# RWKV-5 attention and a two-layer MLP on one core: second MLP product by a seven-product scheme in six of twelve pairs, and joined masks

## The chip, the cores and the metric

The kernel runs on one core of one Trainium2 chip. The metric is device time in microseconds. Before the change, three runs took 173.43, 173.54 and 174.15 us; their median is 173.54 us.

## The reference

Inputs are r, k, v of shape 4 x 8 x 768 x 48 (batch, head, token, channel), a decay w and a bonus u per head and channel, and the MLP's matrices `w_in` (384 x 2048) and `w_out` (2048 x 384). All is float32; the kernel works in bfloat16 with float32 sums.

```python
for t in range(S):                       # S = 768
    cur = einsum('bhd,bhe->bhde', u * k[t], v[t])
    y[t] = einsum('bhd,bhde->bhe', r[t], state + cur)
    state = w * state + einsum('bhd,bhe->bhde', k[t], v[t])
x = y.transpose(0, 2, 1, 3).reshape(3072, 384)
h = x @ w_in                             # 3072 x 2048
out = maximum(0.01 * h, h) @ w_out       # 3072 x 384
```

## The kernel before

The 3072 tokens are cut into 24 stages of 128 tokens; six stages make one batch (NC = 6), so the running state starts anew at stages 0, 6, 12 and 18. Two stages form a pair, and there are twelve pairs, 0 to 11. Work is written as a list of operations with the tiles that each reads and writes (`Sched.add`); each engine plays its own operations in that order, and semaphores are put in between engines where one needs another's result, or where a buffer is still being read.

**What one stage does.** `load_one` (L210) loads r, k and v by DMAs that POOL issues. `prep` (L305, L307) multiplies r and k by tables of powers of the decay on VectorE (DVE), into `qk`; from stage 8 on SP then issues a DMA that transposes `qk` into `tp` (L310), while earlier stages are turned on TensorE (`turn`, L355). `prep2` makes the bonus term: from stage 8 on it multiplies twice and reduces on DVE (L330, L332, L334), and POOL writes two diagonal tiles into `at` (L342); for earlier stages it scales v (`vs`, L325). `a_mm` (L377) multiplies queries and keys into two PSUM banks, one for each half of the heads; `a_mask` puts the part below the diagonal into `at` with one DVE operation for each bank (L387, or L391 as a predicated copy over the diagonal tiles). `kv_mm` (L408) and `state` (L458, or L461 and L463) carry the state on, the latter on DVE. `y_part` (L493) sums everything into the output in small matmuls of 32 columns of the array; for stages below 8, twelve of them add `vs` through the identity. ScalarE (ACT) copies the result into `xT` (L508).

**The MLP.** `g1_pair` (L538) multiplies `w_in` by a pair's `xT`, 256 tokens at a time, in eight groups of six matmuls; ACT applies the leaky maximum and writes `gT` (L544). `g2` (L555) multiplies one stage's `gT` by `w_out`: 16 matmuls of 384 columns into one PSUM bank. ACT copies it out (L561), and SP stores the stage (L563).

**Order.** Stages 0 to 9 and the first pairs of the MLP follow a list written by hand (`ORDER`), in which J is `g1_pair`, H is `g2`, P `prep`, Q `prep2`, A `a_mm`, M `a_mask`, K `kv_mm`, S `state`, Y `y_part`, L the loads. Then a loop runs over m = 3 to 11 (L576 to L604). One turn m holds the eight `g1_pair` of pair m; `prep2` of stages 2m+4 and 2m+5; loads of 2m+8 and 2m+9; `a_mm` and `a_mask` of 2m+4 and 2m+5; `y_part` of 2m+2 and 2m+3; `kv_mm` and `state` of 2m+4 and 2m+5 (not of a batch's last stage); `prep` of 2m+6 and 2m+7; and `g2` of both stages of pair m-1. The two `g2` of pair 11 stand behind the loop.

**PSUM.** There are eight banks of 512 columns, taken round in turn by `next_bank`: a new user of a bank waits until the readers of the user eight banks earlier are done. In the turn m = 5, for example, the sixteen takers before `g2` are eight `g1_pair`, four halves of `a_mm`, two `y_part` and two `kv_mm`, so that the first `g2` gets the bank of the first half of `a_mm(14)`.

Of the kernel before, what the change touches and what calls it, by code (L numbers as in the profile page):

```python
# [5 lines left out]
ALU = mybir.AluOpType  # L6
# [114 lines left out]
def bass_rwkv5_eagle__then__act_leaky_relu_kernel(  # L121
# [32 lines left out]
    qtab = SB("qtab", [128, HD])  # L154
    ktab = SB("ktab", [128, HD])
# [21 lines left out]
    gT = [SB(f"gT{i}", [128, NFB, 256]) for i in range(NG)]  # L177
    out_sb = [SB(f"out_sb{i}", [128, HD], FP32) for i in range(NO)]
    ps = [ctx.enter_context(nc.psum_tensor(f"ps{i}", [128, 512], FP32)) for i in range(8)]
# [22 lines left out]
    def load_one(n, which, pace=()):  # L202
# [3 lines left out]
        if which == "v":  # L206
            dst = v_sb[:, n, :].rearrange("p (h e) -> p h e", e=E)[:, :, 0:D]
        else:
            dst = {"k": k_sb, "r": r_sb}[which][:, n, :].rearrange("p (h d) -> p h d", d=D)
        add("pool", lambda: G.dma_start(dst, src), R=pace, W=[(which, n)], dma=f"{which}{n}")  # L210

# [85 lines left out]
    def k_of(n):  # L297
        return k_sb[:, n, :] if n else k0_f[:, :]

    def r_of(n):  # L300
        return r_sb[:, n, :] if n else r0_f[:, :]
# [12 lines left out]

# [5 lines left out]
    def prep2(n):  # L320
# [8 lines left out]
        else:  # L329
            add("dve", lambda: V.tensor_tensor(ku[i2][:, :], k_of(n), u_tab[:, :], ALU.mult),  # L330
                R=[("k", n), "u_tab"], W=[("ku", i2)])
            add("dve", lambda: V.tensor_tensor(rku[i2][:, :], r_of(n), ku[i2][:, :], ALU.mult),  # L332
                R=[("r", n), ("ku", i2)], W=[("rku", i2)])
# [35 lines left out]
    def a_mm(n):  # L369
        it = n % NTP  # L370
        at_bank[n] = (next_bank(), next_bank())
# [11 lines left out]
    def a_mask(n):  # L383
        for hh in range(2):
            part = at_bank[n][hh][0][:, :].rearrange("p (m i) -> p m i", i=128)
            if n < DIAG:
                add("dve", lambda hh=hh, part=part: V.tensor_tensor(  # L387
# [188 lines left out]
    for m in range(FIRST // 2, NST // 2):  # L576
# [3 lines left out]
        for n in ahead:  # L580
            prep2(n)
# [82 lines left out]
```

## Time and profile before

The profiled execution spans 171.8 us from the first to the last instruction; the median run of 173.54 us lies 1.7 us above that span. The granted clock of TensorE is 1.00 in every stretch up to 158 us.

| what | value |
|---|---|
| median of runs / span of the profiled execution | 173.54 us / 171.8 us |
| busy: PE, DVE, ACT, POOL | 95%, 56%, 54%, 60% of the span |
| second MLP product (L555), 384 matmuls | 64.5 us |
| first MLP product in pairs (L538), 480 matmuls | 54.5 us |
| POOL's diagonal tiles (L342), 32 | 33.8 us, 1081 ns each |
| masks (L391), 32 | 19.8 us, 684 ns each |
| last instruction of DVE | at 138.6 us |
| store of an output stage (192 KB), median to landing | 2.2 us |

In a row of the profile the columns are line, engine, operation, output<-input, shape and count; then the busy time and the mean of one instruction, which can overlap with the next. In a timeline or a chain of waits the first two columns are start and length in us, and a bracket gives the idle time before and what ended it. A matmul's mean length (326 ns at 384 columns) holds its way through the array; what one costs in a stream is seen from a run of many. PE is TensorE's matmuls, PEld its weight loads.

### The profile page before, as it was taken

The numbers are of one execution on the slowest core, as the hardware profiler recorded it, in microseconds if no ns is written. First come the engines' busy times: TensorE is split into PE (matmuls) and PEld (weight loads), VectorE is DVE, ScalarE is ACT, GpSimd is POOL, SyncE is SP. The second block draws the span as 40 slices with busy tenths as digits, with TensorE's granted clock in tenths as the row PEclk, the third lists the DMA queues.
The fourth block names the chain that finished last, engine by engine and source line by source line (L and its number), as shares of the span: only waits on it lengthen the run. The fifth ranks groups of instructions, "written<-read, shape, count | busy, mean of one in ns | idle before, by whom it ended". The sixth has DMA issues, their size and how long they took to land.

```text
span 171.8 us, 5029 instructions
## 1 busy us (share of the span) xinstructions
PE 163.4 (95%) x2179; PEld 122.4 (71%) x2179; DVE 95.7 (56%) x209; ACT 92.5 (54%) x169; POOL 102.7 (60%) x117
## 2 busy tenths in 40 slices
PE   6799999969999989999999999999999999999993
PEld 1578799859666856876877867868868768678661
DVE  7699859550999679079189197296396520000000
ACT  4755698759123841942934934825817718539121
POOL 7999999990379998972993997957207200000000
PEclk9999999999999999999999999999999999999999
DMA  5999999999999999999499499899008011011112
GB/s 98 119 150 157 171 153 173 200 179 144 112 98 240 94 145 126 202 101 116 133 93 138 128 89 143 147 116 217 0 4 214 4 46 46 4 46 50 46 48 92
DMA packets 98970, 19.66 MB, mean 114 GB/s; under 512 B 92290, under 2 KB 98948, under 8 KB 98948
## 3 DMA queue, kind: packets, MB, share of 16 engines
q0 software_dynamic: 76512, 10.03, 89.7%
q1 hardware_dynamic: 21394, 9.11, 27.1%
q8 instruction: 17, 0.28, 0.7%
q10 hardware_dynamic: 1042, 0.20, 0.6%
q14 instruction: 5, 0.04, 0.1%
HBM read 20.45 MB, written 4.72 MB: 146 GB/s over the span
## 4 chain that ended last, share of the span: by engine, by line
PE 76%; DMA 9%; DVE 6%; POOL 6%; issue 2%; ACT 0%; POOLq 0%; ACTq 0%
PE ps L555 30%; PE ps L538 28%; PE ps L521 6%; PE ps L493 6%; DMA tp<-qk 5%; DMA w_in_sb<-in_moe_w_in_dram 4%; PE ps L377 3%; PE ps L408 2%; DVE qk L307 2%; POOL v_sb L210 2%; POOL r_sb L210 2%; POOL k_sb L210 2%; PE ps L355 1%; DVE ku L330 1%; DVE s_tok L334 1%
## 5 line engine op out<-in xcount | busy, mean ns | idle before, releaser
L555 PE MATMUL ps<-w_out_sb,gT 128*128 128x384 bf16 x384 | 64.5, 326 | 0.0
L538 PE MATMUL ps<-xT,w_in_sb 128*128 128x256 bf16 x480 | 54.5, 273 | 0.0
L555 PEld LDWEIGHTS ps<-w_out_sb,gT 128*128 128x128 bf16 x384 | 36.9, 98 | 23.4
L342 POOL TENSOR_TENSOR at<-ident,s_tok 128x512 bf16<-128x512 bf16 x32 | 33.8, 1081 | 30.3 <-DVE s_tok L334 30.3
L544 ACT ACTIVATE gT<-ps 128x512 bf16<-128x512 f32 x80 | 47.8, 597 | 7.0 <-PE ps L538 2.1
L538 PEld LDWEIGHTS ps<-xT,w_in_sb 128*128 128x128 bf16 x480 | 46.7, 98 | 6.4
L561 ACT ACTIVATE out_sb<-ps 128x384 f32<-128x384 f32 x24 | 11.8, 490 | 55.1 <-PE ps L555 55.1
L391 DVE CAST_PREDICATED at<-mask,ps 128x512 bf16<-128x512 uint16 x32 | 19.8, 684 | 27.6 <-PE ps L377 25.3
L210 POOL DMA_DIRECT2D v_sb<-in_v_dram x24 | 22.6, 948 | 0.4 <-issue 0.4
L210 POOL DMA_DIRECT2D k_sb<-in_k_dram x23 | 21.7, 945 | 0.0
L210 POOL DMA_DIRECT2D r_sb<-in_r_dram x23 | 21.4, 932 | 0.0
L508 ACT ACTIVATE xT<-ps 128x384 bf16<-128x384 f32 x24 | 11.0, 490 | 4.8 <-PE ps L493 4.3
L521 PE MATMUL ps<-xT,w_in_sb 128*128 128x128 bf16 x192 | 12.3, 219 | 0.3 <-DMA w_in_sb<-in_moe_w_in_dram 0.3
L493 PE MATMUL ps<-at,v_sb 128*32 128x128 bf16 x384 | 11.9, 224 | 0.0
L521 PEld LDWEIGHTS ps<-xT,w_in_sb 128*128 128x128 bf16 x192 | 11.1, 98 | 1.0 <-DMA w_in_sb<-in_moe_w_in_dram 0.6
L526 ACT ACTIVATE gT<-ps 128x512 bf16<-128x512 f32 x16 | 9.6, 599 | 3.6 <-PE ps L521 3.0
L332 DVE TENSOR_TENSOR rku<-r_sb,ku 128x384 bf16<-128x384 bf16 x16 | 10.8, 674 | 0.5
L387 DVE TENSOR_TENSOR at<-ps,mask 128x512 bf16<-128x512 f32 x16 | 10.3, 682 | 1.3 <-PE ps L377 1.3
L493 PEld LDWEIGHTS ps<-at,v_sb 128*32 128x32 bf16 x384 | 9.1, 98 | 2.0 <-issue 0.5
L366 ACT ACTIVATE tp<-ps 128x512 bf16<-128x512 f32 x15 | 8.2, 596 | 3.8 <-PE ps L355 3.8
L493 PE MATMUL ps<-tp,st 128*32 128x128 bf16 x240 | 10.1, 219 | 0.0
L377 PE MATMUL ps<-tp 48*128 48x128 bf16 x192 | 9.1, 228 | 0.9 <-DMA tp<-qk 0.7
(62 smaller groups left out, 134.5 us busy)
## 6 DMA issues: line engine op xcount, KB each, us to landing
out_dram<-out_sb SPq DMA_DIRECT2D x24, 192.0 KB, 2.2
v_sb<-in_v_dram POOLq DMA_DIRECT2D x24, 96.0 KB, 5.9
r_sb<-in_r_dram POOLq DMA_DIRECT2D x23, 96.0 KB, 5.1
k_sb<-in_k_dram POOLq DMA_DIRECT2D x23, 96.0 KB, 5.0
w_in_sb<-in_moe_w_in_dram POOLq DMA_DIRECT2D x4, 384.0 KB, 7.4
w_out_sb<-in_moe_w_out_dram POOLq DMA_DIRECT2D x4, 384.0 KB, 11.1
tp<-qk SPq DMA_TRANSPOSE x16, 3.4
r_f<-in_r_dram SPq DMA_DIRECT2D x1, 192.0 KB, 3.5
```

Of the source, the lines that this page charges most:

```text
L210: add("pool", lambda: G.dma_start(dst, src), R=pace, W=[(which, n)], dma=f"{which}{n}")
L332: add("dve", lambda: V.tensor_tensor(rku[i2][:, :], r_of(n), ku[i2][:, :], ALU.mult), R=[("r", n), ("ku", i2)], W=[("rku", i2)])
L342: add("pool", lambda hh=hh, s_of=s_of: G.tensor_tensor(at[ia][:, hh, :, :], ident[:, :].unsqueeze(1).to_broadcast([128, NP, 128]), s_of.un ...
L377: last = PE.matmul(at_bank[n][hh][0][:, 128 * p:128 * p + 128], tp[it][rows, NP + p, :], tp[it][rows, p, :], start=True, stop=True)
L391: add("dve", lambda hh=hh, part=part: V.copy_predicated(at[n % NAT][:, hh, :, :], mask[:, :].bitcast(mybir.dt.uint16).unsqueeze(1).to_broa ...
L493: last = PE.matmul(ps_y[32 * q:32 * q + 32, 128 * s:128 * s + 128], a, m, start=first_mm, stop=last_mm)
L508: add("act", lambda: A.activation(xT[m % NX][:, :, 128 * half:128 * half + 128], ps_y[:, 0:HD].rearrange("p (s t) -> p s t", t=128), AF.Copy),
L521: last = PE.matmul(ps_g[:, 128 * f:128 * f + 128], w_in_sb[:, s, 128 * fb:128 * fb + 128], xT[ix][:, s, t], start=s == 0, stop=s == NSL - 1)
L538: last = PE.matmul(ps_g[:, 256 * f:256 * f + 256], w_in_sb[:, s, 128 * fb:128 * fb + 128], xT[ix][:, s, :], start=s == 0, stop=s == NSL - 1)
L544: add("act", lambda: A.activation(gT[ig][:, 2 * j:2 * j + 2, :].rearrange("p f t -> p (f t)"), ps_g[:, :], AF.Prelu, alpha=0.01), R=[key], ...
L555: last = PE.matmul(ps_o[:, 0:HD], gT[ig][:, s, 128 * half:128 * half + 128], w_out_sb[:, s, :], start=s == 0, stop=s == NFB - 1)
L561: add("act", lambda: A.activation(out_sb[io][:, :], ps_o[:, 0:HD], AF.Copy), R=[key], W=[("o", io)])
```

## The change

The second MLP product of a pair is, in blocks, a 2 x 2 matrix product: rows are the pair's two stages (128 tokens each), the inner dimension is cut into two halves of 1024 (`top` and `low`, eight blocks of 128 each), and the 384 output columns into two halves of 192. Done plainly, that is eight block products. For pairs 4, 6, 8, 9, 10 and 11 (`SEVEN`) it becomes seven block products of eight matmuls of 192 columns each, in the manner of Strassen and Winograd:

- `w_sum` makes four sums of blocks of `w_out` once (DVE, 1536 wide, bfloat16), two at the end of turn m = 3 and two at the end of m = 4.
- `g_sum` makes four sums of blocks of a pair's `gT` (DVE, 1024 wide, bfloat16), behind `prep2` in the turn that follows the pair; for pair 11 behind the loop.
- `g2_seven` runs the products in three banks (four for pair 11). One bank is filled, read, and added to again: by ACT (`keep`, a float32 copy of 192 columns) or by DVE (`plus`, a sum of the bank and a kept copy that gives a quarter of the output). Pair 11 has its own order and stores each quarter by itself; the other pairs store whole stages.

Beside this, from stage 8 on `prep` is one DVE operation over r and k together (768 wide); `a_mask` is one operation over both banks of a stage (1024 wide), for which `a_mm` takes two neighbouring banks and skips bank 7 where they would not be neighbours; r and k lie in a ring of 14 stages, so a load waits for the readers of the stage 14 before; and for stages below 8 the twelve small matmuls with `vs` become three over the full array. PSUM is declared as one tensor. The diff, cut to its core (declarations, keys and the output's buffers are left out):

```diff
-    NQK, NTP, NVS, NAT, NT, NX, NG, NO = 6, 6, 6, 6, 6, 3, 3, 4
+    NQK, NTP, NVS, NAT, NT, NX, NG, NO, NRK = 6, 6, 6, 6, 6, 3, 3, 4, 14
     TURNED, DIAG = 8, 8
+    SEVEN = (4,6,8,9,10,11)
+    HF, NH = NFB // 2, HD // 2
     w_in_sb = SB("w_in_sb", [128, NSL, DFF])
     w_out_sb = SB("w_out_sb", [128, NFB, HD])
-    r_sb = SB("r_sb", [128, NST, HD])
-    k_sb = SB("k_sb", [128, NST, HD])
+    rk_sb = SB("rk_sb", [128, NRK, 2, HD])
...
+    tw = [SB(f"tw{i}", [128, HF, NH]) for i in range(4)]
+    gs = [[SB(f"gs{i}_{j}", [128, HF, 128]) for j in range(4)] for i in range(2)]
+    snap = [[SB(f"snap{i}_{j}", [128, NH], FP32) for j in range(4)] for i in range(2)]
...
+    ps_all = ctx.enter_context(nc.psum_tensor("ps_all", [128, 8 * 512], FP32))
+    ps = [ps_all[:, 512 * i:512 * i + 512] for i in range(8)]
...
     def prep(n):
         iq = n % NQK
-        add("dve", lambda: V.tensor_tensor(qk[iq][:, 0:H, 0:D], hd(r_of(n)), hd(qtab[:, :]), ALU.mult),
-            R=[("r", n), "qtab", ("qk0", iq)], W=[("qp", iq)])
-        add("dve", lambda: V.tensor_tensor(qk[iq][:, H:2 * H, 0:D], hd(k_of(n)), hd(ktab[:, :]), ALU.mult),
-            R=[("k", n), "ktab", ("qk0", iq)], W=[("kp", iq)])
         if n >= TURNED:
+            both = rk_sb[:, n % NRK, :, :].rearrange("p w (h d) -> p (w h) d", d=D)
+            by = tab[:, :, :].rearrange("p w (h d) -> p (w h) d", d=D)
+            add("dve", lambda: V.tensor_tensor(qk[iq][:, :, 0:D], both, by, ALU.mult),
+                R=[("r", n % NRK), ("k", n % NRK), "qtab", "ktab", ("qk0", iq)], W=[("qp", iq), ("kp", iq)])
             add("sp", lambda: SP.dma_start_transpose(tp[n % NTP][:, :, :],
                                                      qk[iq][:, :, :].rearrange("p h e -> p (h e)")),
                 R=[("kp", iq), ("qp", iq), ("qk0", iq)], W=[("tp", n % NTP, 0), ("tp", n % NTP, 1)],
                 dma=f"tp{n % NTP}")
+            return
+        add("dve", lambda: V.tensor_tensor(qk[iq][:, 0:H, 0:D], hd(r_of(n)), hd(qtab[:, :]), ALU.mult),
+            R=[("r", n % NRK), "qtab", ("qk0", iq)], W=[("qp", iq)])
+        add("dve", lambda: V.tensor_tensor(qk[iq][:, H:2 * H, 0:D], hd(k_of(n)), hd(ktab[:, :]), ALU.mult),
+            R=[("k", n % NRK), "ktab", ("qk0", iq)], W=[("kp", iq)])
...
     def a_mm(n):
         it = n % NTP
+        if n >= DIAG and taken[0] % 8 == 7:
+            taken[0] += 1
         at_bank[n] = (next_bank(), next_bank())
...
     def a_mask(n):
+        if n >= DIAG:
+            i = at_bank[n][0][1][1]
+            halves = [("at", n % NAT, hh) for hh in range(2)]
+            add("dve", lambda: V.copy_predicated(
+                at[n % NAT][:, :, :, :].rearrange("p two m i -> p (two m) i"),
+                mask[:, :].bitcast(mybir.dt.uint16).unsqueeze(1).to_broadcast([128, H, 128]),
+                ps_all[:, 512 * i:512 * i + 1024].rearrange("p (m i) -> p m i", i=128)),
+                R=[key for _, key in at_bank[n]] + ["mask"] + halves, W=halves)
+            return
...
-                if n < DIAG:
-                    one.append((vs[iv][:, 128 * s + 32 * q:128 * s + 32 * q + 32], ident[:, :]))
...
+                                         start=first_mm and (s == 0 or n >= DIAG),
+                                         stop=last_mm and n >= DIAG)
+            if n < DIAG:
+                for s in range(NSL):
+                    last = PE.matmul(ps_y[:, 128 * s:128 * s + 128], vs[iv][:, 128 * s:128 * s + 128], ident[:, :],
+                                     start=False, stop=s == NSL - 1)
...
+    def w_sum(i):
+        top, low = slice(0, HF), slice(HF, NFB)
+        one, two = slice(0, NH), slice(NH, HD)
+        a, b, op, keys = [
+            (w_out_sb[:, top, two], w_out_sb[:, top, one], ALU.subtract, []),
+            (w_out_sb[:, low, two], tw[0][:, :, :], ALU.subtract, [("tw", 0)]),
+            (w_out_sb[:, low, two], w_out_sb[:, top, two], ALU.subtract, []),
+            (w_out_sb[:, low, one], tw[1][:, :, :], ALU.subtract, [("tw", 1)]),
+        ][i]
+        add("dve", lambda: V.tensor_tensor(tw[i][:, :, :], a, b, op),
+            R=[("wout", j) for j in range(4)] + keys, W=[("tw", i)])
+
+    def g_sum(m, i):
+        ig, x = m % NG, gs[m % 2]
+
+        def block(r, c):
+            return gT[ig][:, HF * c:HF * c + HF, 128 * r:128 * r + 128]
+
+        def held(r, c):
+            return [("gT", ig, r, j) for j in range(4 * c, 4 * c + 4)]
+
+        a, b, op, keys = [
+            (block(1, 0), block(1, 1), ALU.add, held(1, 0) + held(1, 1)),
+            (x[0][:, :, :], block(0, 0), ALU.subtract, [("gs", m % 2, 0)] + held(0, 0)),
+            (block(0, 0), block(1, 0), ALU.subtract, held(0, 0) + held(1, 0)),
+            (block(0, 1), x[1][:, :, :], ALU.subtract, [("gs", m % 2, 1)] + held(0, 1)),
+        ][i]
+        add("dve", lambda: V.tensor_tensor(x[i][:, :, :], a, b, op), R=keys, W=[("gs", m % 2, i)])
+
+    def g2_seven(m):
+        ig, i2 = m % NG, m % 2
+        final = m == NST // 2 - 1
+        banks = [next_bank() for _ in range(4 if final else 3)]
+        top, low = slice(0, HF), slice(HF, NFB)
+        one, two = slice(0, NH), slice(NH, HD)
+
+        def product(where, left, right, first, last):
+            ps_o, key = banks[where]
+            if isinstance(left, int):
+                lhs, reads = gs[i2][left], [("gs", i2, left)]
+            else:
+                r, c = left
+                lhs = gT[ig][:, HF * c:HF * c + HF, 128 * r:128 * r + 128]
+                reads = [("gT", ig, r, j) for j in range(4 * c, 4 * c + 4)]
+            if isinstance(right, int):
+                rhs = tw[right]
+                reads = reads + [("tw", right)]
+            else:
+                rhs = w_out_sb[:, right[0], right[1]]
+                reads = reads + [("wout", i) for i in range(4)]
+
+            def emit():
+                for s in range(HF):
+                    done = PE.matmul(ps_o[:, 0:NH], lhs[:, s, :], rhs[:, s, :], start=first and s == 0,
+                                     stop=s == HF - 1, skip_group_check=not (first and last))
+                return done
+
+            add("pe", emit, R=reads, W=[key])
...
+        def keep(where, i):
+            ps_o, key = banks[where]
+            add("act", lambda: A.activation(snap[i2][i][:, :], ps_o[:, 0:NH], AF.Copy), R=[key], W=[("snap", i2, i)])
...
+        def plus(where, i, r, c, after=()):
+            ps_o, key = banks[where]
+            io, cols = (2 * m + r) % NO, (one, two)[c]
+            add("dve", lambda: V.tensor_tensor(out_sb[io][:, cols], ps_o[:, 0:NH], snap[i2][i][:, :], ALU.add),
+                R=[key, ("snap", i2, i), *after], W=[("o", io, c)])
+            store(r, c)
...
+        if not final:
+            product(0, (0, 0), (top, one), True, False)
+            keep(0, 0)
+            product(1, 0, 0, True, False)
+            keep(1, 1)
+            product(0, 1, 1, False, False)
+            keep(0, 2)
+            product(2, (0, 1), (low, one), True, True)
+            plus(2, 0, 0, 0)
+            product(0, 2, 2, False, False)
+            plus(0, 1, 1, 1)
+            product(1, 3, (low, two), False, True)
+            plus(1, 2, 0, 1)
+            product(0, (1, 1), 3, False, True)
+            plain(0, 1, 0)
+            return
+        product(0, (0, 0), (top, one), True, False)
+        keep(0, 0)
+        product(3, 2, 2, True, False)
+        keep(3, 3)
+        product(2, (0, 1), (low, one), True, True)
+        plus(2, 0, 0, 0)
+        product(3, (1, 1), 3, False, True)
+        product(1, 0, 0, True, False)
+        add("dve", lambda: V.tensor_tensor(snap[i2][1][:, :], banks[1][0][:, 0:NH], snap[i2][3][:, :], ALU.add),
+            R=[banks[1][1], ("snap", i2, 3)], W=[("snap", i2, 1)])
+        product(0, 1, 1, False, True)
+        keep(0, 2)
+        plus(0, 1, 1, 1, after=[("snap", i2, 2)])
+        plus(3, 2, 1, 0)
+        product(1, 3, (low, two), False, True)
+        plus(1, 2, 0, 1)
...
+    def second(m):
+        if m in SEVEN:
+            g2_seven(m)
+        else:
+            g2(2 * m)
+            g2(2 * m + 1)
+
     for m in range(FIRST // 2, NST // 2):
         for j in range(8):
             g1_pair(m, j)
         ahead = [n for n in (2 * m + 4, 2 * m + 5) if n < NST]
         for n in ahead:
             prep2(n)
+        if m - 1 in SEVEN:
+            for i in (0, 1, 3, 2):
+                g_sum(m - 1, i)
         for n in (2 * m + 8, 2 * m + 9):
             if n < NST:
                 load_stage(n, pace=[("pace", 2 * m, 0)])
@@ -600,10 +752,13 @@
         for n in (2 * m + 6, 2 * m + 7):
             if n < NST:
                 prep(n)
-        g2(2 * m - 2)
-        g2(2 * m - 1)
-    g2(NST - 2)
-    g2(NST - 1)
+        if m < 5:
+            w_sum(2 * m - 6)
+            w_sum(2 * m - 5)
+        second(m - 1)
+    for i in (2, 0, 1, 3):
+        g_sum(NST // 2 - 1, i)
+    second(NST // 2 - 1)
```

More of the change, by code (lines that the diff above doesn't have):

```diff
@@ L153, in bass_rwkv5_eagle__then__act_leaky_relu_kernel @@
     r0_f = SB("r0_f", [128, HD], FP32)
-    qtab = SB("qtab", [128, HD])
-    ktab = SB("ktab", [128, HD])
+    tab = SB("tab", [128, 2, HD])
+    qtab, ktab = tab[:, 0, :], tab[:, 1, :]
     tcol = SB("tcol", [128, 1], FP32)
@@ L208, in load_one @@
         else:
-            dst = {"k": k_sb, "r": r_sb}[which][:, n, :].rearrange("p (h d) -> p h d", d=D)
-        add("pool", lambda: G.dma_start(dst, src), R=pace, W=[(which, n)], dma=f"{which}{n}")
+            dst = {"k": k_sb, "r": r_sb}[which][:, n % NRK, :].rearrange("p (h d) -> p h d", d=D)
+        key = (which, n if which == "v" else n % NRK)
+        add("pool", lambda: G.dma_start(dst, src), R=pace, W=[key], dma=f"{which}{n}")
     def load_stage(n, pace=()):
@@ L330, in prep2 @@
             add("dve", lambda: V.tensor_tensor(ku[i2][:, :], k_of(n), u_tab[:, :], ALU.mult),
-                R=[("k", n), "u_tab"], W=[("ku", i2)])
+                R=[("k", n % NRK), "u_tab"], W=[("ku", i2)])
             add("dve", lambda: V.tensor_tensor(rku[i2][:, :], r_of(n), ku[i2][:, :], ALU.mult),
-                R=[("r", n), ("ku", i2)], W=[("rku", i2)])
+                R=[("r", n % NRK), ("ku", i2)], W=[("rku", i2)])
             add("dve", lambda: V.tensor_reduce(s_tok[i2][:, :], hd(rku[i2][:, :]), AX.X, ALU.add),
```

40 lines of the change are left out of this document (25 added, 15 removed).

## The prediction

> **What bounds the kernel now.** I read the page first. Its slices show TensorE (PE) at nine tenths nearly everywhere, VectorE (DVE) idle at the end, GpSimd (POOL) and the DMA engines full in the first half.
>
> ```profile
> PE   6799999969999989999999999999999999999993
> DVE  7699859550999679079189197296396520000000
> POOL 7999999990379998972993997957207200000000
> L555 PE MATMUL ps<-w_out_sb,gT 128*128 128x384 bf16 x384 | 64.5, 326 | 0.0
> ```
>
> Next I read the chain that ended last, in order of time, at two places.
>
> ```profile
> 34.22 1.51 issue
> ...
> 53.12 8.41 DMA tp<-qk
> 61.53 0.14 issue
> 61.66 0.40 PE ps L377 x8
> ...
> 87.74 5.20 PE ps L555 x32
> 92.94 5.24 PE ps L538 x48
> ...
> 158.45 10.41 PE ps L555 x64
> ```
>
> From 61.66 to 168.86 the chain is PE alone: the second product of a pair of stages takes 5.20 us, the first 5.24. Before that, PE stands twice: at 34.2 for 1.5 us with no releaser (an instruction fetch is under way), and at 60.9 for 0.73 us for the transposed stage 11. So from 61 us on PE work removed is time removed, as long as no other engine becomes late. The third view, the timeline of DVE and POOL in iteration m=5, says who could be.
>
> ```profile
> 80.29 0.35 DVE L330 TENSOR_TENSOR ku<-k_sb,u_tab 128x384 bf16<-128x384 bf16 x1
> 80.67 1.08 DVE L332 TENSOR_TENSOR rku<-r_sb,ku 128x384 bf16<-128x384 bf16 x1
> 81.79 0.55 DVE L334 TENSOR_REDUCE s_tok<-rku 128x8 f32<-128x384 bf16 x1
> 86.45 2.48 DVE L391 CAST_PREDICATED at<-mask,ps 128x512 bf16<-128x512 uint16 x4 [4.11 <-PE ps L377]
> 80.46 4.20 POOL L342 TENSOR_TENSOR at<-ident,s_tok 128x512 bf16<-128x512 bf16 x4 [4.20 <-DVE s_tok L334]
> ```
>
> DVE has a hole of 4.11 us (82.3 to 86.4), where the change puts its sums. But rku, 0.36 us one stage earlier, takes 1.08 us: it ends 0.21 us after the first POOL product, as if the two could not run together. Reductions and sums with a PSUM operand beside POOL keep their length.
>
> **Durations.** The PE step is 5.20/32 = 162.5 ns for 384 columns, 5.24/48 = 109.2 for 256, 1.34/24 = 55.9 for 128: straight, so 82.5 ns for 192. DVE bf16 from SBUF: 0.35 us (384 wide), 0.42 (512), so 0.55 per 1000; back to back 0.27 at 384, hence steps of 0.47 (768, joined prep), 0.60 (1024, a sum of gT) and 0.87 (1536, a sum of w_out). A mask of 512 takes steps of 0.60 (2.48 us for four); at 1.0 per 1000 (PSUM rows of 384 and 512: 0.55, 0.68) the joined one takes 1.13, ending 1.21 after its start. Of 192 columns, DVE's PSUM sum takes 0.36 us and ACT's copy 0.33.
>
> **Seven products.** 56 matmuls x 82.5 = 4.62 us in place of 5.20: 0.58 saved a pair, 3.48 for six. The row for this pace is L521: 24 matmuls of 128 columns, each with its own weight load, in 1.34 us, so loads keep up. Against it stands the Trainium skill, TensorE: Matmul & The Clock Gate, section "Back-to-back issue gap": with weight loads a sustained step is about 81 ns at 128 columns and 131 at 512. By that, 192 columns would take an estimated 89 ns, a pair would save 0.2 us in place of 0.58, and the sum would be near 174.6; the trace's 55.9 ns at 128 speaks against it.
>
> **The turns of a bank.** In six pairs one bank is filled, read, and filled on, three times, with one other product (0.66 us) between. From the start of the first product: last matmul issued 0.58, ends 0.83; reader starts 0.05 later; ACT copy 0.33; PE resumes 0.10 to 0.19 after an ACT instruction and 0.06 after a DVE one (gaps in this trace), and its first matmul follows some 0.04 later. That is 1.35 to 1.44 for ACT against 1.32 without a wait, and about 1.34 for DVE. I take 0.07 for each of two ACT turns and 0.01 for DVE: 0.15 a pair, 0.90 in all (bounds 0.3 to 2.2).
>
> **Joined masks.** Counting next_bank through the program, the first product behind the masks took, in m=5 before, the bank of half 0 of the first masked stage (free at 87.14, wanted at 87.53). Now that bank is free only when the joined mask ends: start + 1.21 + 0.06. By the traced starts: m=6 98.62 gives 99.89 against 99.70 (0.19 late), m=8 likewise 0.18, m=4 0.03, m=7 0.02. Together 0.42 lost, though DVE itself saves 0.14 an iteration; the joined preps save it another 0.14.
>
> **The sums in the hole.** In m=4 two sums of w_out (1.74 us) stand behind the preps; less 0.28 by joining they move the start of prep2 in m=5 from 79.05 to 80.52. Its last reduction leaves DVE free 3.2 us later, at 83.7. POOL's four products (1.05 each, 81.9 on) then alternate with the four sums: each sum waits for the running product, runs 0.55, and holds the next one up. First sum done 84.7, then cycles of 1.45 (qk, ku beside POOL: cycle 1.12 with 0.20 of own work; 0.33 more here): 86.1, 87.6, and the last, free of POOL, 88.1. The masks start at 88.05 in place of 86.45. The first product's bank is free at 89.3 (wanted 87.53); masks end 90.3, states 92.15 (1.84 as now), preps 93.1, the DVE sums that release bank 0 for the seventh product 93.7. It starts at 93.8 and ends at 94.5: the pair takes 6.91 us in place of 5.20. So m=5 loses 6.91 - 5.20 = 1.71; beside its 0.58 gain and 0.15 of turns, the late DVE costs 2.14. Without the alternation (sums at 0.60 to 0.70 each) the masks start on time, and the pair takes 5.3.
> The same reckoning in m=7, with no w_out sums ahead: sums done at 111.9, masks due at 112.7 (both shifted by what PE lost before): nothing. In m=9: done 135.70, due 135.46, the first bank free at 136.97 against 136.54: 0.43. In m=10 and m=11 DVE has nothing else. Sums of m=11 need the last gT (159.1) and follow the pair-10 sums; the first is done 0.3 us before its product. POOL's loads for stages 18, 19 leave 2.4 us later; their preps come 11 us after that.
>
> **Early part.** The new 128-wide s-term products replace 12 small matmuls by three: 12 x 16.8 ns against 3 x 55.9, 0.03 a stage, given back by the 0.09 that PE loses at each change of tile shape: nothing. But 18 PE instructions less a stage move the fetch stall at 34.2. Fetches there come 3 to 5 us late behind loads; 256 instructions now carry more work. Bounds: all 1.67 us gone, or the stall only elsewhere (0); the transposes of stages 8, 9 land at 51.24 and 52.12, just before their use, which eats part. I take 0.80. The joined preps get ahead of POOL's products (the second halves, 1.20 us each at 45.8 and 49.3, waited for them): prep 11 ends 0.7 us earlier, so its transpose is issued ahead of two loads, and PE's wait of 0.73 goes. Next late would be the mask of stage 11, which POOL's product ending at 61.0 holds; it has a microsecond.
> The ring of 14 adds waits to POOL's loads only on readers 14 stages back, long done. **The end**: last eviction 0.36 by DVE for 0.49 by ACT, 0.14 gained; the half-size store I count like the whole (2.2 us).
>
> **Sum.** -3.48 +0.90 +0.42 +2.14 +0.43 -0.80 -0.73 -0.14 = -1.26 us on the span of 171.8, so 170.5; the median run, 173.54, lies 1.7 above that span, mine at 172.3.
>
> **Rivals.**
> No alternation: sums slip between POOL's products, or POOL yields. The same-length reductions beside POOL speak for it, rku and qk against. m=5 then gains 1.60, m=9 0.24: 170.4. Chance 0.15.
> Early gains fail: the fetch stall only moves and transpose 11 lands late behind loads anyway (8.41 us now). 172.3 + 1.53 = 173.8, no change. Speaks for it: DMA at nine tenths there. Chance 0.25.
> Slower, by one mechanism: the turns. All six pairs accumulate into a bank just read; if a turn costs 0.17 us or more rather than 0.05 (18 turns, 2.2 us more) the kernel ends above 174.4; at 0.20 it is 175.0. The 0.19 us gap behind one gT eviction before L555 points there, most gaps (0.10) don't. Chance 0.12.
> Sums at one element a cycle (vs at L325 takes 0.55 at 384, with an f32 operand): 0.53 more each. w_out sums then start m=5 1.6 later still, its sums 2.1, m=7 1.4, m=9 2.1: 179. All operands are bf16 in rows of 128 or 192, like prep's rows of 48, which run at 0.27. Chance 0.04.
> Weight loads not overlapped (98 ns each, the page's PEld row): 5.5 us a pair, 177.5; L521 speaks against. Chance 0.02; the skill's milder figure is above.
> It doesn't multiply less: the diff issues 7 x 8 matmuls of 192 columns; excluded.
>
> **Chances.** My forecast 0.42: mostly 171.4 to 172.9. What a measurement can tell here is about 0.5%, 0.87 us: faster is under 172.67. Forecast (0.35 of its 0.42) and no alternation (0.15), with 0.05 from early failure partly true, make faster 0.55; same gets 0.07 and 0.20, 0.27; slower 0.18 (turns 0.12, slow sums 0.04, loads 0.02). Range: 170.0 (no alternation and more of the fetch stall gone) to 174.3 (early gains fail and turns at 0.08).
>
> **What will show it.** Steps of 82.5 ns in the products; about 4.8 us for pairs 9 to 11 and 6.9 for pair 4; gT sums of 1.4 us beside POOL and 0.7 without in m=10; masks at 88 rather than 86.4 (shifted); LDWEIGHTS gaps before third, fifth and seventh products; PE's waits at 34.2 and 60.9. A sum of gT of 0.7 us beside POOL, or a gap over 0.15 at each turn, would prove me wrong.

## The result, and the profile after

The changed kernel took 172.78 us (median of ten runs, 172.22 to 172.95); beside it on the same chip the kernel before took 174.12 us (ten runs, 173.43 to 175.13). The ratio is 0.9926, with a 95% interval of 0.9900 to 0.9953. The forecast, 172.3 for a before of 173.54, was a ratio of 0.9929. The profiled execution of the changed kernel took 172.86 us and spans 171.1 us, 0.7 less than the span of before.

The page of the changed kernel, two rows of its slices and two groups of instructions:

```profile
PE   6799999999999999999969999999999999999992
...
DVE  7689766752998779389999479989399967053272
...
L354 POOL TENSOR_TENSOR at<-ident,s_tok 128x512 bf16<-128x512 bf16 x32 | 36.8, 1177 | 28.3 <-DVE s_tok L346 28.3
...
L639 PE MATMUL ps_all<-tw,gs 128*128 128x192 bf16 x144 | 13.8, 246 | 0.0
```

PE has one slice under nine tenths in the middle (the 6, at about 86 us); before it had none there, but two near 35 and 60 us. DVE now works to the end. POOL's diagonal tiles, untouched by the change, went from 1081 to 1177 ns each. The products of two sums, one of `gT` and one of `w_out` (the 144 matmuls of the last row), wait for nothing; where the others wait is shown below. Lines have moved: L558 is `g1_pair`, L575 `g2`, L639 a product of `g2_seven`, L613 `g_sum`, L401 the joined mask, L391 `a_mm`, L508 and L513 `y_part` in columns and over the full array, L425 `kv_mm`, L670 `plus`, L647 `keep`.

The chain that ended last, of the changed kernel, where before it showed 1.51 us of "issue" at 34.22:

```profile
35.29 0.19 PE ps_all L425 x4
35.48 1.31 PE ps_all L558 x12
```

The four `kv_mm` now run on without a gap. The wait for transpose 11 is gone too: the 16 `a_mm` of m = 3 are one piece of 0.55 us. What came in its place is in the same view, in m = 5, where the chain of before was PE alone:

```profile
84.99 0.57 PE ps_all L391 x16
...
86.47 0.68 DVE gs L613
87.15 2.26 DVE at L401 x2
...
92.11 0.62 DVE out_sb L670 x2
...
92.78 0.83 PE ps_all L639 x8
```

PE waits for the masks, which wait for the last sum of gT; and again, before the seventh product, for the sums that free its bank. The timeline of PE gives the sizes (start, length, then in the bracket the idle time and its releaser):

```profile
88.34 0.83 PE L639 MATMUL ps_all<-w_out_sb,gT 128*128 128x192 bf16 x8 [1.63 <-DVE at L401]
...
92.78 0.83 PE L639 MATMUL ps_all<-tw,gT 128*128 128x192 bf16 x8 [0.30 <-DVE out_sb L670]
```

Counted from start to start, which leaves out a matmul's way through the array, PE lost 1.79 us before the first product (due at 86.55) and 0.47 before the seventh; the pair took 86.55 to 93.45, 6.90 us.

**The kernel cut by turns.** Below, "full pace" is the time from PE's first matmul to the moment from which matmuls of 128 columns follow one another every 56 ns, where before they took 107 (the granted clock of 1.00 that the page gives for that early time doesn't show this), "to J3" from that matmul to the first `g1_pair` of m = 3, "m = 3" to "m = 10" from one turn's first `g1_pair` to the next one's, "rest" from the first `g1_pair` of m = 11 to the last matmul's end, and "landing" from there to the last store's landing. All are us, from the traces. The two kernels were also profiled a second time (the runs e9 and e10 below).

| | full pace | to J3 | m=3 | 4 | 5 | 6 | 7 | 8 | 9 | 10 | rest | landing | total |
|---|---|---|---|---|---|---|---|---|---|---|---|---|---|
| before | 12.40 | 53.55 | 13.07 | 12.33 | 12.17 | 12.16 | 12.33 | 12.17 | 12.17 | 11.44 | 15.80 | 2.50 | 169.70 |
| before again | 14.86 | 54.23 | 12.55 | 12.33 | 12.17 | 12.16 | 12.33 | 12.17 | 12.16 | 11.44 | 15.80 | 2.49 | 169.85 |
| after | 14.71 | 53.27 | 12.34 | 12.34 | 13.86 | 12.34 | 11.85 | 12.34 | 12.10 | 10.93 | 14.75 | 2.72 | 168.82 |
| after again | 12.94 | 52.37 | 12.34 | 12.34 | 13.87 | 12.34 | 11.85 | 12.34 | 12.11 | 10.93 | 14.74 | 2.73 | 167.94 |

From m = 4 on, the turns repeat to 0.02 us. The start doesn't: the moment of full pace is a matter of the execution, not of the kernel. A pair of traces with about the same moment (after and before again, or after again and before) differs by 1.0 and by 1.8 us in all.

### The profile page after: what moved, and what is told of

It is laid out like the page before. It is cut to its first block, busy times and chain, and to the rows that moved or that the text cites. A ratio compares the mean times of both kernels' runs of the same rounds, so it can differ in the third digit from the quotient of the medians.

```text
span 171.1 us, 5225 instructions
## 1 busy us (share of the span) xinstructions
PE 162.4 (95%) x2251; PEld 132.0 (77%) x2251; DVE 124.1 (73%) x225; ACT 94.0 (55%) x180; POOL 105.7 (62%) x117
## 4 chain that ended last, share of the span: by engine, by line
PE 85%; DVE 5%; DMA 3%; POOL 2%; issue 2%; DVEq 0%; ACT 0%; POOLq 0%
PE ps_all L558 31%; PE ps_all L575 19%; PE ps_all L639 14%; PE ps_all L541 7%; PE ps_all L508 5%; PE ps_all L391 4%; DMA rk_sb<-in_k_dram 3%; PE ps_all L425 2%; DVE at L401 2%; POOL rk_sb L217 2%; PE ps_all L367 1%; PE ps_all L513 1%; DVE out_sb L670 1%; DVE at L409 1%; POOL v_sb L217 1%
## 5 line engine op out<-in xcount | busy, mean ns | idle before, releaser
L558 PE MATMUL ps_all<-xT,w_in_sb 128*128 128x256 bf16 x480 | 54.5, 273 | 0.0
L354 POOL TENSOR_TENSOR at<-ident,s_tok 128x512 bf16<-128x512 bf16 x32 | 36.8, 1177 | 28.3 <-DVE s_tok L346 28.3
L558 PEld LDWEIGHTS ps_all<-xT,w_in_sb 128*128 128x128 bf16 x480 | 46.7, 98 | 5.9
L564 ACT ACTIVATE gT<-ps_all 128x512 bf16<-128x512 f32 x80 | 47.7, 597 | 6.1 <-PE ps_all L558 1.7
L575 PE MATMUL ps_all<-w_out_sb,gT 128*128 128x384 bf16 x192 | 32.6, 326 | 0.0
L401 DVE CAST_PREDICATED at<-mask,ps_all 128x1024 bf16<-128x1024 uint16 x16 | 18.8, 1218 | 12.2 <-PE ps_all L391 12.2
L575 PEld LDWEIGHTS ps_all<-w_out_sb,gT 128*128 128x128 bf16 x192 | 18.3, 98 | 12.0
L217 POOL DMA_DIRECT2D rk_sb<-in_k_dram x23 | 21.7, 942 | 0.0
L217 POOL DMA_DIRECT2D rk_sb<-in_r_dram x23 | 21.4, 930 | 0.0
L670 DVE TENSOR_TENSOR out_sb<-ps_all,snap 128x192 f32<-128x192 f32 x19 | 6.3, 353 | 15.8 <-PE ps_all L639 15.1
L639 PE MATMUL ps_all<-tw,gs 128*128 128x192 bf16 x144 | 13.8, 246 | 0.0
L541 PE MATMUL ps_all<-xT,w_in_sb 128*128 128x128 bf16 x192 | 13.0, 225 | 0.0
L541 PEld LDWEIGHTS ps_all<-xT,w_in_sb 128*128 128x128 bf16 x192 | 11.7, 101 | 0.5 <-issue 0.2
L639 PEld LDWEIGHTS ps_all<-tw,gs 128*128 128x128 bf16 x144 | 12.1, 98 | 0.0
L639 PE MATMUL ps_all<-w_out_sb,gT 128*128 128x192 bf16 x96 | 9.9, 246 | 1.9 <-DVE at L401 1.9
L647 ACT ACTIVATE snap<-ps_all 128x192 f32<-128x192 f32 x18 | 5.9, 330 | 10.4 <-PE ps_all L639 10.4
L546 ACT ACTIVATE gT<-ps_all 128x512 bf16<-128x512 f32 x16 | 9.6, 599 | 3.8 <-PE ps_all L541 3.1
```

The costliest lines, as they stand in the source:

```text
L217: add("pool", lambda: G.dma_start(dst, src), R=pace, W=[key], dma=f"{which}{n}")
L354: add("pool", lambda hh=hh, s_of=s_of: G.tensor_tensor(at[ia][:, hh, :, :], ident[:, :].unsqueeze(1).to_broadcast([128, NP, 128]), s_of.un ...
L401: add("dve", lambda: V.copy_predicated(at[n % NAT][:, :, :, :].rearrange("p two m i -> p (two m) i"), mask[:, :].bitcast(mybir.dt.uint16). ...
L541: last = PE.matmul(ps_g[:, 128 * f:128 * f + 128], w_in_sb[:, s, 128 * fb:128 * fb + 128], xT[ix][:, s, t], start=s == 0, stop=s == NSL - 1)
L546: add("act", lambda: A.activation(gT[ig][:, 4 * grp:4 * grp + 4, t], ps_g[:, :].rearrange("p (f t) -> p f t", t=128), AF.Prelu, alpha=0.01 ...
L558: last = PE.matmul(ps_g[:, 256 * f:256 * f + 256], w_in_sb[:, s, 128 * fb:128 * fb + 128], xT[ix][:, s, :], start=s == 0, stop=s == NSL - 1)
```

## The experiments

The theory is that of the prediction: the sums of gT alternate with POOL's products, which makes m = 5 lose what six cheaper pairs gain; the early gain comes from the full-array products with `vs`, which take instructions out of PE's stream; the joined masks cost PE what the bank order says. The rivals: m = 5 is late only because the sums of `w_out` stand ahead of it (no contention); the early gain comes from elsewhere, the joined preps or luck; the scheme's products gain less than 0.58 us a pair, or lose it again in the turns of a bank. e1 to e4 shared one chip, e5 to e8 another, e9 and e10 a third; each ratio is to the kernel before, run beside it.

**e1, the fifth pair done plainly.**

```diff
-    SEVEN = (4,6,8,9,10,11)
+    SEVEN = (6,8,9,10,11)
```

> Pair 4 goes back to two plain products; its sums of gT go, the sums of w_out and all else stay. Theory (in turn m=5 DVE is late, because its four sums alternate with POOL's products): pair 4 now costs 1.69 us more than a plain pair, so turn m=5 (J5 start to J6 start, 13.86 us in the changed kernel) falls to about 12.35, 0.2 above the 12.17 of before because of the joined mask, and the kernel gains about 1.5 us: 171.3, ratio 0.984. Rival (m=5 is late for another reason, the sums of w_out or the joined operations): the turn stays near 13.9 and the time near 172.8.

It took 170.23 us (before there 173.0), a ratio of 0.9856 (0.9821 to 0.9891), below the interval of the changed kernel. The turn m = 5 fell from 13.86 to 12.33 us. The chain of this kernel in m = 5 is PE alone again:

```profile
85.44 0.45 PE ps_all L425 x8
85.89 5.37 PE ps_all L575 x32
```

One thing came unasked: m = 9 also fell, from 12.10 to 11.65. The scheme takes three banks for a pair where two `g2` take two, so with pair 4 plain every later taker stands one bank elsewhere, and the first product of pair 8 takes the bank of the last `g1_pair` of m = 9, which ACT has long emptied, instead of that of a masked stage. The sums of that turn are as long as before (1.42 us beside POOL), but PE doesn't ask for the masks' banks first.

**e2, all four sums of `w_out` in m = 3.** There DVE has time, and the sums of gT in m = 5 start earlier.

```diff
-        if m < 5:
-            w_sum(2 * m - 6)
-            w_sum(2 * m - 5)
+        if m == 3:
+            for i in range(4):
+                w_sum(i)
```

> All four sums of w_out stand at the end of turn m=3; everything else as in the changed kernel. Theory: DVE enters turn m=5 1.74 us earlier, its sums, though still 7.6 us long with prep2 beside POOL, end at about 85.3, just as the masks of stage 14 are due (85.4); then the pair waits only for the joined mask (0.2) and some 0.45 for its last sum, turn m=5 takes 12.1 to 12.3 us in place of 13.86, and the kernel comes to about 171.1, ratio 0.983. In m=3 DVE has 3.1 us free before the masks of m=4, so nothing is lost there. Rival (the alternation with POOL itself, wherever it falls, costs PE the time): turn m=5 stays above 13 us and the time above 172.

It took 171.98 us, 0.9922 (0.9890 to 0.9954): m = 5 fell to 13.01, half of what was expected. The sums of `w_out` did leave; DVE came to `prep2` 1.74 us earlier. But POOL, then still at its loads, started its diagonal tiles in the middle of it. The timeline of this kernel, POOL's two rows, then two of DVE's:

```profile
79.30 2.09 POOL L354 TENSOR_TENSOR at<-ident,s_tok 128x512 bf16<-128x512 bf16 x2
82.28 2.87 POOL L354 TENSOR_TENSOR at<-ident,s_tok 128x512 bf16<-128x512 bf16 x2 [0.89 <-DVE s_tok L346]
```

```profile
79.39 2.22 DVE L344 TENSOR_TENSOR rku<-rk_sb,ku 128x384 bf16<-128x384 bf16 x1
...
86.22 2.34 DVE L401 CAST_PREDICATED at<-mask,ps_all 128x1024 bf16<-128x1024 uint16 x2
```

The `rku` issued 0.09 us after POOL's first product waited for both of POOL's products, 2.22 us for an operation that takes 0.36 alone. The masks start at 86.2, still after their due time of 85.4. So the sums of `w_out` make up about half of what m = 5 lost, and the meeting with POOL remains when they are gone; the expectation that they were nearly all of it was wrong.

**e3, the twelve small products with `vs` back** in the stages below 8.

```diff
+                if n < DIAG:
+                    one.append((vs[iv][:, 128 * s + 32 * q:128 * s + 32 * q + 32], ident[:, :]))
...
-            if n < DIAG:
-                for s in range(NSL):
-                    last = PE.matmul(ps_y[:, 128 * s:128 * s + 128], vs[iv][:, 128 * s:128 * s + 128], ident[:, :],
-                                     start=False, stop=s == NSL - 1)
```

> For stages below 8 the twelve small matmuls with vs return in place of the three over the full array. Theory: the three cost two changes of tile shape of about 0.1 us each where two stages follow one another, 0.6 to 0.7 us in all up to 52 us, so that is gained; but the 18 PE instructions a stage return too, and with them the instruction-fetch wait of 1.67 us at 34 us, which the changed kernel does not have. Both: 173.7, ratio 0.998, with the wait seen at about 34 us. Rival (the wait went by chance of the DMA queues and not by the count of instructions): no wait, 172.1, ratio 0.988.

It took 173.4 us, 1.0019 (0.9982 to 1.0056). The wait is back at its old place, inside the same four `kv_mm`, in the chain of this kernel:

```profile
34.66 0.15 PE ps_all L425 x3
34.80 1.25 issue
```

At the same moment of full pace as the changed kernel (14.69 us) its J3 starts 0.46 us later. That is less than the 1.25 of the wait, since the full-array products aren't free: each change between 32-column pieces and the full array costs time, and two stages one behind the other have three such changes more. Two stages took 1.32 us in one run of 80 matmuls and take 1.55 in the changed kernel; the chains of e3 and of the changed kernel:

```profile
30.40 1.32 PE ps_all L510 x80
```

```profile
30.79 0.50 PE ps_all L508 x28
31.29 0.27 PE ps_all L513 x3
31.57 0.51 PE ps_all L508 x28
32.07 0.27 PE ps_all L513 x3
```

By the ratios of the runs e3 lies 1.6 us above the changed kernel, by the intervals at least 0.5; what it has beyond the 0.46 isn't explained.

**e4, a mask for each bank again**, the banks still neighbours.

```diff
...
-                mask[:, :].bitcast(mybir.dt.uint16).unsqueeze(1).to_broadcast([128, H, 128]),
-                ps_all[:, 512 * i:512 * i + 1024].rearrange("p (m i) -> p m i", i=128)),
...
+                mask[:, :].bitcast(mybir.dt.uint16).unsqueeze(1).to_broadcast([128, NP, 128]), part),
...
```

(that is: one predicated copy for each half `hh`, of `part`, its own bank)

> Two masks a stage again, one for each bank, still in neighbouring banks. Theory: the first product of a pair takes the bank of the first half, which now comes free 0.5 us earlier; the waits of 0.16 us in turns m=3, m=6 and m=8 and the 0.44 us in m=9 go, m=5 stays bound by DVE (0.1 to 0.2 us later). Sum about -0.8 us: 172.0, ratio 0.988. Rival (DVE's relief by joining matters more than the bank): m=5 and m=9 become longer and the time stays or grows above 172.8.

It took 171.92 us, 0.9946 (0.9930 to 0.9963), which the runs can't tell from the changed kernel. By turns the forecast held where it was made: m = 3, 6 and 8 fell by 0.17 to 0.18 each. But m = 9 fell by 0.23 where 0.44 was expected, and m = 5 and 7 rose by 0.27 and 0.13, because four masks take DVE longer than two and the sums that free the seventh product's bank stand behind them. The turns' sum fell by 0.38. In the chain of this kernel PE still waits in m = 5, but only for half a mask:

```profile
86.05 0.68 DVE gs L610
86.73 0.61 DVE at L405
...
87.38 3.49 PE ps_all L636 x40
```

**e5, the sums of gT ahead of `prep2`**, timed once: the same sums without POOL beside them.

```diff
+        if m - 1 in SEVEN:
+            for i in (0, 1, 3, 2):
+                g_sum(m - 1, i)
         for n in ahead:
             prep2(n)
-        if m - 1 in SEVEN:
-            for i in (0, 1, 3, 2):
-                g_sum(m - 1, i)
```

> The four sums of gT stand ahead of prep2 in their turn, so that POOL's products, which need prep2, come after them. Theory (each sum waits for a POOL product): in turns m=5, m=7 and m=9 the sums now take 0.69 us each, about 2.5 us in all, as they do in m=10 where POOL is idle, and not 0.94, 1.41, 1.42 and 0.68; what is late next is POOL itself, whose last product ends near 87.5 in m=5, where the second mask wants it at 86.6. Turn m=5 about 13.1 us (13.86 in the changed kernel). Rival (the sums are long by themselves, for their operands): they keep 0.94 to 1.42 us and m=5 stays at 13.9.

It took 173.19 us (before there 173.2). Two rows of DVE and one of POOL in its timeline:

```profile
81.03 0.69 DVE L613 TENSOR_TENSOR gs<-gs,gT 128x1024 bf16<-128x1024 bf16 x1
...
88.61 1.22 DVE L401 CAST_PREDICATED at<-mask,ps_all 128x1024 bf16<-128x1024 uint16 x1 [0.78 <-POOL at L354]
```

```profile
84.38 4.20 POOL L354 TENSOR_TENSOR at<-ident,s_tok 128x512 bf16<-128x512 bf16 x4 [6.00 <-DVE s_tok L346]
```

The four sums took 0.68, 0.69, 0.69 and 0.69 us in place of 0.94, 1.41, 1.42 and 0.68, and POOL's four products 4.20 in place of 5.09: both lengthen only when they meet. The turn gains only 0.39 us by it (13.47; 13.1 was expected), for POOL starts 2.65 us later in the turn and then holds the masks, which write over its tiles. The kernel as a whole gained nothing: its full pace came at 16.79 us, and J3 0.8 us later than in the changed kernel.

**e6, all else but the scheme**: `SEVEN` empty, and no `w_sum` or `g_sum`.

```diff
-    SEVEN = (4,6,8,9,10,11)
+    SEVEN = ()
```

> No pair by seven products, no sums; joined masks and preps, ring and full-array s-terms stay. By the turns of J: 0.17 more than before wherever the first plain product gets the bank of the masks just made (m=3, 4, 5, 7, 8 by the order of banks), so 12.34 in place of 12.17; the end as before (15.80 us from J11 to the last matmul); the fetch wait of 1.67 us gone. Theory: the seven products as placed are worth only some 0.6 us of the whole, so this is 173.3, ratio 0.996. Rival (the seven products make all of the gain): ratio 1.00 or above.

It took 172.93 us, 0.9981 (0.9952 to 1.0010); 0.996 lies in the interval, and so does no change. Its turns are 12.34, 12.34, 12.33, 12.17, 12.50, 12.34, 12.16 and 11.44: m = 3 has lost its wait as in the changed kernel, and m = 5, 7 and 8 pay 0.16 to 0.17 each for the joined masks. In m = 7 the prediction had 0.02, but for the changed kernel's order of banks; in the order of e6 PE waits twice there, once for each bank of a masked stage. J3 starts at 52.78 with full pace at 13.84, between the changed kernel's 52.37 at 12.94 and 53.27 at 14.71: the early part is the same.

From J3 to the landing it takes 115.92 us, the changed kernel 115.55 and 115.57 in its two traces, e1 113.54. So by the traces the scheme is worth 0.4 us in six pairs and 2.4 in five, and most of what the change gained came from the early part and m = 3. The prediction's terms say the same: -3.48 +0.90 +2.14 +0.43 -0.14 is -0.15 for the scheme, and +0.42 -0.80 -0.73 is -1.11 for the rest. The medians of the runs say the reverse, 0.3 us gained by e6 and 1.3 by the change; but the two intervals meet at 0.8 us, so the runs settle no share, and the split rests on single traces.

**e7, what the runs so far pointed to**: e1 and e4 together, the small products back in stages 6 and 7 only, and of the four last half stores the third issued by ACT.

```diff
+                if 6 <= n < DIAG:
+                    one.append((vs[iv][:, 128 * s + 32 * q:128 * s + 32 * q + 32], ident[:, :]))
...
-            if n < DIAG:
+            if n < 6:
...
-                add("sp", lambda: SP.dma_start(out[128 * n:128 * n + 128, cols], out_sb[io][:, cols]),
+                eng, queue = ("act", A) if len(landed) == 3 else ("sp", SP)
+                add(eng, lambda: queue.dma_start(out[128 * n:128 * n + 128, cols], out_sb[io][:, cols]),
```

> Pair 4 plain, masks apart, small vs matmuls again in stages 6 and 7 alone, and the last store from ACT's queue. Theory, from the runs so far: pair 4 plain gave 1.5 us in turn m=5 and 0.45 in m=9; masks apart give 0.17 in each of m=3, 4, 5 and 8 and cost 0.13 in m=7; the two s-terms give back 0.3 at 50 us without bringing the fetch wait at 34 us back (it lies before them); the last store starts 0.4 us earlier. Together 1.2 us below the run with pair 4 plain: ratio about 0.979. Rival (each gain only moves the next wait): the ratio stays at 0.985.

It took 170.45 us (before there 173.2), 0.9834 (0.9794 to 0.9874), the lowest ratio here; but its interval overlaps e1's, so that it beats both kernels is shown, and that it beats e1 is not. The traces, at the same moment of full pace (13.06 and 13.13 us), put it 1.0 us below e1: 0.32 to J3, 0.53 in the turns, and 0.17 at the landing, where 0.4 was expected. The ratio that was expected, 0.979, lies just outside the interval, the rival's 0.985 inside.

**e8, the scheme in the last four pairs only.**

```diff
-    SEVEN = (4,6,8,9,10,11)
+    SEVEN = (8,9,10,11)
```

> Only the last four pairs by seven products. Theory: against the changed kernel turn m=5 falls by 1.5 us and m=9 by 0.45 (its first product then gets a bank of g1_pair and no mask's), and turn m=7 grows by 0.35 to 0.5: 171.1 on the scale of 172.78, ratio 0.987. So of the two further pairs, the fifth costs more than the seventh gains. Rival (the further pairs both pay): slower than the changed kernel, ratio above 0.993.

It took 171.16 us, 0.9883 (0.9847 to 0.9920). Against it, pairs 4 and 6 of the changed kernel cost 1.52 us in m = 5, 0.18 in m = 6 and 0.45 in m = 9, and gain 0.66 in m = 7: 1.5 us lost on balance by the traces. With e1 between the two, pair 6 alone is worth its 0.5 us, and pair 4 costs 2.0.

**e9 and e10, the changed kernel and the kernel before again**, unedited, for the start.

> The changed kernel as it is, profiled and timed a second time. In the profiles so far the matmuls change from steps of 107 ns to 56 ns (128 columns) at 12.4 to 16.8 us after the first matmul, and the start of J3 moves by half of that. Theory (this moment belongs to the run and not to the kernel): another moment here than the 14.71 us of the first profile, the start of J3 shifted by half the difference from 53.27, the turns from J3 on equal within 0.03 us, and no wait at 34 us. Rival (the changed program brings the late moment with it): again 14.7 and 53.3.

> The kernel before, profiled a second time. Theory: the instruction-fetch wait of 1.67 us at 34 us and the wait for the transposed stage 11 at 61 us belong to the program and are there again, to within some tenths; the moment of full matmul pace differs from 12.40 us and the start of J3 (53.55) moves by half of that. Rival (the fetch wait is chance): no wait over 0.3 us near 34 us.

The changed kernel took 172.3 us (before there 173.28), 0.9948 (0.9898 to 0.9999); the kernel before, run once, 173.72. The turns came out as in the table above. For before, J3 moved by 0.68 us with a full pace 2.46 us later, not by half of that. The wait inside `kv_mm` is in both executions of before and in e3 (1.51, 1.42 and 1.25 us), and in neither of the changed kernel. The wait for transpose 11 isn't so firm: 0.73 us in one trace of before and 0.2 in the other, where PE reached it later. No run undid the joined preps alone, so that they removed it stays argued.

## Why the prediction was right, step by step

The sum was right in its result, and in most of its terms; three were off, the turns, the early part and the end, and they offset one another. That it came within 0.1 us of the measured gain is therefore partly luck. Predicted and measured, in us, the measured from the table of turns (after less before):

| step | predicted | measured |
|---|---|---|
| early part, to J3 | -0.80 | -0.28; -1.0 to -1.2 at an equal moment of full pace |
| m = 3: wait for transpose 11 | -0.73 | -0.73; -0.21 against before again |
| m = 4, 6, 8: joined masks | +0.03, +0.19, +0.18 | +0.01, +0.18, +0.17 |
| m = 5: pair 4, late DVE and mask | +1.71 | +1.69 |
| m = 7: pair 6 | -0.41 | -0.48 |
| m = 9: pair 8, late mask | 0.00 | -0.07 |
| m = 10: pair 9 | -0.43 | -0.51 |
| rest: pairs 10 and 11 | -0.86 | -1.05 |
| landing | -0.14 | +0.22 |
| all | -1.26 | -0.88; -1.0 and -1.8 at an equal moment; -1.29 by the ratio of the runs |

**Seven products: right.** The products of pair 9 start at 148.31, 148.97, then (the fourth) 150.29, 150.96 and 151.62: 0.66 us for eight matmuls, 82.5 ns each, weight loads and all, as taken from the rows of 128, 256 and 384 columns. The figure of the Trainium skill that was weighed against it (TensorE: Matmul & The Clock Gate, section "Back-to-back issue gap"), from which 89 ns was estimated, was not met by this stream.

**Turns of a bank: mis-sized on the safe side.** Forecast 0.15 a pair, measured 0.06. The two ACT turns cost nothing, though the interval came out as 1.32 to 1.33 us, as forecast; the wait that shows is the one for `plus`, ahead of the seventh product: 0.055 us, and 0.079 in m = 7. That is why m = 7, 9, 10 and the rest each came out 0.07 to 0.1 lower a pair.

**Sums in the hole: right, by its mechanism.** The prediction had the masks 1.60 us late, the first product waiting 1.77, the seventh late again, and 6.91 for the pair; the runs had 1.64 (87.07, where 86.45 less the 1.02 that PE was ahead is due), 1.79, 0.47 and 6.90. The timeline of the changed kernel shows the alternation that the row `rku` had announced, DVE's sums and POOL's products:

```profile
82.71 0.94 DVE L613 TENSOR_TENSOR gs<-gT 128x1024 bf16<-128x1024 bf16 x1
83.69 1.41 DVE L613 TENSOR_TENSOR gs<-gs,gT 128x1024 bf16<-128x1024 bf16 x1
85.13 1.42 DVE L613 TENSOR_TENSOR gs<-gT,gs 128x1024 bf16<-128x1024 bf16 x1
86.47 0.68 DVE L613 TENSOR_TENSOR gs<-gT 128x1024 bf16<-128x1024 bf16 x1
87.07 2.34 DVE L401 CAST_PREDICATED at<-mask,ps_all 128x1024 bf16<-128x1024 uint16 x2
```

```profile
80.91 5.09 POOL L354 TENSOR_TENSOR at<-ident,s_tok 128x512 bf16<-128x512 bf16 x4 [3.35 <-DVE s_tok L346]
```

POOL's second, third and fourth product end at 83.11, 84.55 and 86.00, and each of the first three sums ends 0.55 us after one of them; the last, alone, takes 0.68, and those of m = 10, with no POOL, 0.68 to 0.69. e5 takes the meeting away and all eight get their own length back, so this cause is shown, not only argued. The Trainium skill (SBUF — State Buffer, section "Who interferes with whom") has a DVE instruction with two SBUF inputs contend with a GpSimd instruction that reads SBUF, through ports that the two share under an exclusive lock; the 0.69 us alone and 1.41 beside POOL agree.

**Joined masks: right where counted, one place missed.** m = 4, 6 and 8 came out to 0.02. Missed was m = 3: there the second product waits for the joined mask of stage 10, 0.17 us by e4, which the wait for the transpose had covered. The measured -0.73 of that turn holds it: the wait for the transpose alone was worth 0.90 there, 13.07 less the 12.17 of a turn without waits.

**Fetch stall: the sign right, the size by two errors.** I took half of 1.67 us. All of the wait went, in both traces of the changed kernel, and e3 brings it back with the small products, so the instructions taken out of PE's stream are what moved it. In the three traces that have it, the wait stands ahead of the same instruction, by the traces' count the 1218th of PE's matmuls and weight loads; in the changed kernel that one starts at 39.5 us, without a wait. So it goes with a place in the stream and not with a moment; that PE waits there for instructions to be fetched stays inferred, for the trace names no releaser. But the line on the full-array products, "0.03 a stage, given back by the 0.09 that PE loses at each change of tile shape: nothing", was no zero: by its own terms it is 0.06 lost in each of eight stages, and where two stages follow each other there are three more changes. Against e3, stages 0, 2 and 3, each by itself, lost 0.01 to 0.12 us, stages 4 and 5 took 1.55 for 1.32 and stages 6 and 7 1.39 for 1.06, and it was some 0.8 in all (1.25 of wait back, 0.46 lost). Of 1.67 that leaves 0.9, near my 0.80 by luck.

**The end: wrong.** Forecast 0.14 gained, measured 0.22 lost. The last eviction is indeed 0.35 us by DVE, but it is the third of three. The chain of the changed kernel's end:

```profile
158.40 8.66 PE ps_all L639 x104
...
167.09 0.34 ACT snap L647
...
167.51 0.62 DVE out_sb L670 x2
168.13 0.27 DVEq L766
```

Three sums queue on DVE behind ACT's `snap` of bank 0 (167.09), the first of them needing it, so the last result is ready at 168.40, 0.65 us after the last matmul; and four half stores stand in one queue on SP, the last issued 0.35 us after its data. I had priced the last instruction and not the queue in front of it.

**The rivals.** "No alternation" (170.4) fell with the sums of 1.41 us. "Early gains fail" (173.8) fell with the wait gone in both traces; the wait for transpose 11 can be small, though. "Turns of 0.17" and slow sums fell with 0.055 and 0.69 us. What I hadn't asked is whether pair 4 belongs in the scheme at all: by my own terms it gained 0.58 - 0.15 and cost 2.14, and e1 is that subtraction done. Nor did I see how little the scheme was worth in sum, though the terms were there.

## What to carry to other kernels

When work is moved to an engine's idle time, read what its neighbour does in that time: sums that fit a 4.1 us hole at 0.69 us each didn't fit at 1.41, and one pair in six lost more than three gained. Price each use of a scheme in its own place, and leave out the uses that lose: five pairs beat six by 2.0 us in the traces, by 1.2 in the ratios of the runs. Where banks or buffers go round in turn, a part that takes one more shifts every later wait, so recount them after each edit.

## What the runs showed of the hardware

**A waiting DVE operation can lose twice.** In e2, `rku`, issued 0.09 us into a POOL product, waited for that one and the next (2.22 us, alone 0.36), whereas the sums of gT got in between two products each time. What decides it wasn't tried.

**The moment of full pace differs between executions of one kernel**: 12.40 and 14.86 us after the first matmul in before, 14.71 and 12.94 in the changed kernel, 16.79 in e5. In the timeline it is seen as twelve matmuls of 128 columns at two paces, here of the changed kernel:

```profile
14.46 1.49 PE L541 MATMUL ps_all<-xT,w_in_sb 128*128 128x128 bf16 x12
...
17.65 0.83 PE L541 MATMUL ps_all<-xT,w_in_sb 128*128 128x128 bf16 x12
```

In the changed kernel J3 comes about 0.5 us later for each us of delay (52.37 at 12.94, 53.27 at 14.71), in the kernel before 0.28 (53.55 at 12.40, 54.23 at 14.86); so a difference of 1 us between two single profiles can be this alone, and spans were compared only at like moments. Why it differs stays open.

**A change of tile shape on PE costs 0.09 to 0.11 us** between the 32-column pieces and the full array, whichever way: in the changed kernel at 31.2 and 31.5 us the first matmul behind a change starts 0.15 us after the one before, where a step takes 0.05 to 0.06. So six full-array matmuls in pieces of their own cost more than the 24 small ones they replace (1.55 against 1.32 us).
